# A fused attention, routing and expert kernel: VectorE's order in a pair of blocks, shared value copies, early transposes, a held routing

## The chip, the cores and the metric

The kernel runs on one core of a Trainium2 chip. The core has five engines that run beside each other: TensorE (PE in the profile, with its weight loads as PEld), VectorE (DVE), ScalarE (ACT), GpSimd (POOL) and SyncE (SP, which here issues transfers). [...] The metric is device time in microseconds, the median of several executions. [...]

## What is computed

Three stages, one after the other:

```python
scores = q @ k.T / 8 + bias            # 4 batches x 8 heads, 768 rows, head size 64
keep   = (first 8 keys) | (own and 95 keys before)
x      = softmax(where(keep, scores, -1e9)) @ v        # as 3072 rows of 512

logits = x @ w_gate                    # 8 experts
order  = argsort(-logits.flatten())    # greedy: best pair first,
...                                    # each expert takes 384 rows
y[mask_e] = relu(x[mask_e] @ w1[e]) @ w2[e]

out = relu(y @ w_in)**2 @ w_out        # 512 -> 2048 -> 512
```

All of it in float32. In the expert stages each operand is split into a high and a low part, and three products take the place of one.

## The kernel before

**Attention.** `attention` goes through 48 pairs of units (4 batches, 4 pairs of heads, 6 blocks of 128 rows; a unit is one block of one pair of heads). The loop `for p in range(NP)` is software pipelined by hand: what it writes down is the order on every engine, since nothing reorders it later. In pair p, with u = 2p: `qk` forms the scores of units u and u+1 on TensorE (L288); `smax` (L298, two instructions per unit) adds the bias and takes the row minimum on VectorE; `sexp` (L306) takes the exponentials on ScalarE; `tr_pe` and `tr_ev` (L315, L320) transpose those of the pair before on TensorE and copy them out of PSUM on ScalarE, in two PSUM buffers `pt0` and `pt1`; `av` (L331) multiplies those of two units earlier with the values into the one PSUM buffer `px0`; and `av_ev` (L336) copies that into `xT` on VectorE.

Tasks are hung into the pairs by tables: `PEF` and `PEL` on TensorE, `DV` on VectorE, `D` for stores. In six pairs for each of the first three batches, `nat_pe` transposes a block of `xT` back (L377) into the bank `mi`, `nat_ev` scales it on VectorE (L380), and `nat_st` stores 128 finished rows of x to `xd` in HBM. Four other pairs of a batch hold the gate logits (`gate_mm` to `gate_red`). `side` is called twice at the end of a pair: it advances the conversion of the last stage's weights, which arrive as 64-bit numbers (`convert`: two GpSimd instructions L928 and L930, two VectorE instructions L932 and L934 for each half matrix), and the preparation of the routing (`prepare`, L579 to L588). VectorE's order in a pair is thus: `smax` twice, the value copy, the pair's other tasks, `side`.

**Routing.** `Router.stage` picks the 384 rows of one expert: it finds a threshold by rounds of compare and count (VectorE compares into `r_ge`, TensorE counts into `r_ps`), then turns the chosen rows into a list of indices: `onehot` on VectorE (tile `r_O`, shown as `c_q<-prow,r_sb`), `place` on TensorE (shown as `r_ps<-va,c_q`). Stage 0 runs alone, ahead of the experts; stages 1 to 7 run beside them.

**Experts.** `ffn` gathers the rows of an expert (`c_xg<-xd,idx`), transposes them (`xtp`), splits them into high and low parts (`parts`: ScalarE casts, VectorE subtracts, tile `c_XT`), and runs the expert (`hg`, `y`) and the last stage (`hg`, `o`) on TensorE, weights being split by ScalarE (`wh`) and GpSimd (`wl`). From stage 0 on, the order on each engine is set while the program is built: `Sched` holds generators that yield the engine they want next, or a function that must become true first, and `Clock` keeps an estimate of when each engine is free (`free`) and when a tile is there (`there`). All these instructions carry line L77. The last batch's six blocks of rows are `tail` tasks of this scheduler: each makes its transposes (into `s0`, `s1`), scales them with eight ScalarE instructions (`xn`) and stores them, between the rounds of routing stage 0.

Of the kernel before, what the change touches and what calls it, by code (L numbers as in the profile page):

```python
# [6 lines left out]
FT = mybir.dt.float32  # L7
# [3 lines left out]
PELAG, PEL = 1.6, 2  # L11
# [106 lines left out]
class Sched:  # L118
# [34 lines left out]
    def run(self, until=None):  # L153
        while self.tasks and not (until and until()):
            best = None
            hold = HOLD if self.busy() else HOLD0
            S, U = [], []
            self.moved = False
            for t in list(self.tasks):
                if t not in self.tasks: continue  # L160
                s = self.start(t)
                if s:
                    S.append((t, s[0], s[1]))
                    U.append(S[-1])

                    if isinstance(t[3], str) and ">" in t[3]: U.append((t, "DVE", s[1] + float(t[3].split(">")[1])))
            if not S:
                assert self.moved, [(t[2].__name__, t[2].gi_frame.f_lineno) for t in self.tasks]
                continue
            for t, eng, s in S:  # L170

                p = t[5] if eng == "PE" else t[0]
                held = (eng != "PE" or not self.busy()) and any(e == eng and u[0] < p and s <= q < s + hold for u, e, q in U)
                key = (held, round(s/0.05), p, t[1])
                if best is None or key < best[0]: best = (key, t)
            self.advance(best[1])
# [6 lines left out]
BIG = 3.0e38  # L183
MASK8 = -8.0e9
FAR = 2.0**43
ND = 1
def first_keys(n_global):

    return 8*max((n_global + 7)//8, 1)
# [17 lines left out]
def tags(name, n):  # L207
    return tuple(f"{name}{i}" for i in range(n))

def attention(tc, sb, pp, q, k, v, wgb, xd, L, n_global, n_local, ident, prepare, beside=()):  # L210
# [4 lines left out]
    nc = tc.nc  # L215
    V, ACT, G, PE, SP = nc.vector, nc.scalar, nc.gpsimd, nc.tensor, nc.sync
    B, HP, NB = 4, 4, 6
# [28 lines left out]
    own, g = rel[:, W-128:W], n_global  # L246
# [15 lines left out]
    T0 = sb.tile([128, 8, 128], FT, "T0")  # L262
# [14 lines left out]
    st, XT, PX = {}, {}, {}  # L277
# [56 lines left out]
    def av_ev(p, copy=V.tensor_copy):  # L334
        b, hp, i = units[2*p]
        copy(XT[b][:, hp, i*128:i*128+256], PX[0])  # L336
    PEF, PEL, DV, D = {}, {}, {}, {}
    def at(where, t, f, *a):
        where.setdefault(t, []).append((f, a))
    GM = {}  # L340
# [20 lines left out]
    def gate_red(b, i0, n, tag="gt"):  # L361
        t = sb.tile([128, n*HP, 2, 8], FT, "gt", (tag,))
        p = GM.pop((b, i0)).rearrange("p i (c a e) -> p (i c) a e", c=HP, e=8)[:, :, 0:2]
        R = RC[:, b, i0:i0+n].rearrange("p i (c a) -> p (i c) a", c=HP)
        V.tensor_tensor(t, p, R[:, :, :, None].to_broadcast([128, n*HP, 2, 8]), op=OP.mult)
        i0 += b*NB
        V.tensor_reduce(L[:, i0:i0+n], t.rearrange("p (i c) a e -> p i e (c a)", c=HP), axis=AX.X, op=OP.add)
        if b < B-1: ready.append((i0, n))
    def parts():
        while True:  # L370
            part = ready.pop(0) if ready else None
            if part == (): return
            yield part
    def nat_pe(b, i, nc=nc):
        GM[3] = pp.tile([128, 512], FT, "nat", ("mi",) if b < B-ND else ("s0", "s1"))
        for hp in range(HP):
            nc.tensor.transpose(GM[3][:, hp*128:hp*128+128], XT[b][:, hp, i*128:i*128+128], ident)  # L377
    def nat_ev(b, i):
        x = GM['x', b, i] = sb.tile([128, 8, 64], FT, "xn", tags('wo', 3))
        V.tensor_tensor(x, GM[3].rearrange("p (h d) -> p h d", h=8), RC[:, b, i, :, None].to_broadcast([128, 8, 64]), op=OP.mult)  # L380
    def nat_act(b, i, p, nc=nc):
        GM['x', b, i] = sb.tile([128, 8, 64], FT, "xn", tags('wo', 3))
        for h in range(8):
            nc.scalar.activation(GM['x', b, i][:, h], p[:, h*64:h*64+64], AF.Copy, scale=RC[:, b, i, h:h+1])
# [3 lines left out]
    for b in range(B - 1):  # L388
        t0 = 12*b + 14
        for f in range(2):  # L390
            d = t0 + 2*f
            if f == 0: at(DV, d, recip, b, 0, NB)
            at(PEL, d, gate_mm, b, 3*f, 3, "mi"); at(DV, d, gate_ev, b, 3*f, 3)
            at(PEF, d+1, gate_tr, b, 3*f, 3, "mi"); at(DV, d+1, gate_red, b, 3*f, 3)
        for i in range(NB if b < B-ND else 0):
            d = t0 + 4 + i
            at(PEF, d, nat_pe, b, i); at(DV, d, nat_ev, b, i); at(D, d, nat_st, b, i)
    for h in range(2, 8): at(DV, h-2, table, h)
    prep = prepare(parts())
    def side(t):  # L400
        for g, n, t0 in beside:
            if t >= t0 and t % n == 0: next(g, None)
        next(prep, None)
    def run(tasks, p):
        for f, a in tasks.get(p, ()): f(*a)
    for p in range(NP):
        u = 2*p
        qk(u)
        qk(u+1)
        n = p // 3  # L410
        if p % 3 == 2 and n + 3 < NQ: load_qk(n+3)
        if p >= 1:
            tr_pe(u-2)
            tr_pe(u-1)
        run(PEF, p)
        smax(u)
        sexp(u)
        if p >= 1: tr_ev(u-2)
        if p >= 2:
            av(u-4)  # L420
            av(u-3)
            if p % 3 == 1 and n + 1 < NQ and n >= 1: load_v(n+1)
        smax(u+1)
        sexp(u+1)
        if p >= 1: tr_ev(u-1)
        run(PEL, p)
        if p >= 2: av_ev(p-2)
        run(DV, p)
        run(D, p)
        side(u)  # L430
        side(u+1)

    b, u = B - 1, 2*NP
    tr_pe(u-2)
# [13 lines left out]
    gate_tr(b, 0, 4, "s0")  # L448
    gate_ev(b, 4, 2, "gs", ACT.copy)
    gate_tr(b, 4, 2, "s2")  # L450
    gate_red(b, 0, 4, "T0")
    next(prep, None)
    gate_red(b, 4, 2)
    ready.extend([(b*NB, NB), ()])
    for _ in prep: pass

    def rows(b, i):
        def steps(nc):
            yield "PE"
            nat_pe(b, i, nc)  # L460
            p = GM[3]
            yield "ACT"
            nat_act(b, i, p, nc)
            yield "SP"
            nat_st(b, i, nc)
        return steps
    return [rows(b, i) for b in range(B-ND, B) for i in range(NB)]

SENT = -1.0e29
BIG = 3.0e38  # L470
# [5 lines left out]

ONE23, MASK = 0x4b000000, 0xffffffff
WMODE = (2,3,4,5,6)

class Router:  # L480

# [109 lines left out]
    def stage(self, s, wp, ps, idx, eidx):  # L591
# [235 lines left out]
        for i, g in enumerate(gs):  # L827
            for h in g:
                onehot(h)
                if h < g[-1] or s == 0 and h < 1: yield ("DVE", sb)  # L830
            if s == 0 and i < 1: continue
            if s == 0: g = gs[i-1]
            yield ("PE", Os[g[-1]], va)
            for h in g: place(h)
            if i < len(gs) - 1: yield ("DVE", sb)
# [121 lines left out]
def ffn(tc, pools, router, ident, xd, wab, wov, wol, out, tail, wih, wil):  # L957
# [58 lines left out]
    def routing(s):  # L1016
        idx[s] = sb.tile([128, 3], I32, "idx", tags("idx", 8))
        eidx[s] = sb.tile([1, 1], I32, "eidx", tags("eidx", 8))
        for r in router.stage(s, wp, rps, idx[s], eidx[s]):
            if r == "e": known.add(s)  # L1020
            elif r == "idx": done.add(s)
            elif r == "soon": soon.add(s)
            else: yield r
        if s + 1 < NE: S.add(routing(s+1), PR[s+1], -1)
# [270 lines left out]
    def rows(g):  # L1295
        yield from g
        n["rows"] += 1
# [177 lines left out]
```

## Time and profile before

| | us |
|---|---|
| median of 3 runs | 1094.42 (1093.69 to 1094.96) |
| the profiled execution's own time | 1095.79 |
| its span, first to last instruction | 1094.0 |
| TensorE busy | 1039.1 (95%) |
| VectorE busy | 717.7 (66%) |
| ScalarE busy | 427.7 (39%) |
| GpSimd busy | 414.9 (38%) |

The profiled execution took 1.79 us more than its span and 1.37 us more than the median. TensorE's share is high throughout, but matrix instructions overlap and their ends are modelled, so a busy TensorE need not be one at its peak. The stages lie as follows: attention until about 181 us, the last blocks and routing stage 0 until about 218.5 us, the gather and the first split until 230 us, and then the eight experts until 1085 us, with the last rows written by 1094 us.

### The profile page before, as it was taken

The page shows a single profiled execution, that of the slowest core. Times are in us where ns is not written, and L with a number is a line of the kernel's source. Part 1 is how long each engine was busy: PE and PEld are TensorE (multiplying, and loading weights), DVE is VectorE, ACT ScalarE, POOL GpSimd, SP SyncE. Part 2 cuts the span into 40 slices and gives each one's busy share as a digit, 9 for nine tenths or more (in the row PEclk, how much of TensorE's full clock was granted, in tenths as well). Part 3 has the DMA queues.
Part 4 walks back from the last instruction along what each step waited for, and adds up shares of the span by engine and source line. Part 5 has one row for each costly group of instructions (what it writes and reads, how often), then busy time and mean ns, then how long its engine had stood idle before and what let it go on. Part 6 is the DMA issues. An engine that isn't in the chain of part 4 may idle for free.

```text
span 1094.0 us, 19130 instructions
## 1 busy us (share of the span) xinstructions
PE 1039.1 (95%) x6599; PEld 919.8 (84%) x6599; DVE 717.7 (66%) x2633; ACT 427.7 (39%) x1087; POOL 414.9 (38%) x458
## 2 busy tenths in 40 slices
PE   8999897589999999999999999999999999999997
PEld 5666665479888988998999889989988999899996
DVE  6888887664489868878887788778876122232322
ACT  7877775533344332332233223322332233223221
POOL 2645550274264443434344335433542355006001
PEclk9999999599999999999999999999999999999999
DMA  8879863652232232323332333223322234123021
GB/s 297 310 271 348 281 245 134 219 163 92 87 125 85 80 126 87 106 72 102 96 107 78 97 87 106 86 88 97 117 87 76 88 116 144 59 62 123 29 68 58
DMA packets 53043, 139.53 MB, mean 128 GB/s; under 512 B 6225, under 2 KB 6609, under 8 KB 52945
## 3 DMA queue, kind: packets, MB, share of 16 engines
q1 hardware_dynamic: 49104, 125.72, 34.2%
q0 software_dynamic: 3840, 12.59, 3.5%
q8 instruction: 52, 0.85, 0.3%
q14 instruction: 47, 0.38, 0.1%
HBM read 117.31 MB, written 20.97 MB: 126 GB/s over the span
## 4 chain that ended last, share of the span: by engine, by line
PE 69%; DVE 10%; issue 2%; ACT 1%; DMA 0%; POOL 0%; POOLq 0%; DVEq 0%; ACTq 0%
PE hg L77 33%; PE o L77 21%; PE y L77 12%; DVE r_ge L77 3%; PE r_ps L77 2%; DVE c_q L77 2%; DVE r_tc L77 1%; DVE r_t L77 1%; DVE va L77 0%; DMA c_xg<-xd,idx 0%; DVE r_th L77 0%; DVE r_pre L77 0%; DVE r_fc L77 0%; DVE c_XT L77 0%; PE xtppt L77 0%
## 5 line engine op out<-in xcount | busy, mean ns | idle before, releaser
L77 PE MATMUL hg<-c_XT,wi 128*128 128x384 f32 x1536 | 291.8, 338 | 0.0
L77 PEld LDWEIGHTS hg<-c_XT,wi 128*128 128x128 f32 x1536 | 270.5, 188 | 9.4
L77 POOL TENSOR_TENSOR wl<-c_T,wh 128x512 fp32r<-128x512 f32 x128 | 167.8, 1326 | 104.5 <-ACT wh L77 104.2
L77 ACT ACTIVATE c_gs<-hg 128x384 f32<-128x384 f32 x128 | 62.8, 491 | 291.9 <-PE hg L77 291.9
L77 DVE TENSOR_SCALAR_CACHE_REDUCE r_ge<-r_wv,r_th 128x192 bf16<-128x192 f32 x350 | 143.8, 411 | 9.5
L77 DVE SCALAR_TENSOR_TENSOR c_q<-hg,c_gs 128x384 f32<-128x384 f32 x112 | 62.3, 556 | 123.5 <-ACT c_gs L77 123.5
L77 PE MATMUL hg<-c_XT,wh 128*128 128x384 f32 x512 | 134.4, 344 | 2.7 <-DVE c_XT L77 2.4
L306 ACT ACTIVATE P<-ns,nm 128x232 f32<-128x232 f32 (+1 forms) x192 | 89.4, 467 | 44.9 <-DVE nm L298 44.6
L77 PE MATMUL o<-wol,c_k 128*128 128x512 f32 x264 | 104.4, 395 | 0.0
L77 PEld LDWEIGHTS hg<-c_XT,wh 128*128 128x128 f32 x512 | 93.4, 190 | 5.3 <-DVE c_XT L77 4.1
L77 ACT CAST wh<-c_T 128x512 fp32r<-128x512 f32 x128 | 75.8, 617 | 38.8 <-DMA c_T<-in_wab 28.5
L77 POOL DMA_INDIRECT out<-c_xg,idx x24 | 23.7, 986 | 168.4 <-DVE c_xg L77 151.3
L77 PE MATMUL hg<-c_XT,wl 128*128 128x384 f32 x256 | 86.7, 339 | 0.0
L77 POOL TENSOR_TENSOR c_q<-c_q,c_q 128x384 fp32r<-128x384 f32 x30 | 31.4, 1045 | 119.2 <-ACT c_q L77 73.8
L77 PE MATMUL y<-c_k,wh 128*128 128x384 f32 x256 | 71.8, 341 | 0.0
L315 PE MATMUL pt<-ident,P 128*128 128x128 f32 x352 | 57.2, 290 | 13.0 <-ACT PT L320 12.8
L315 PEld LDWEIGHTS pt<-ident,P 128*128 128x128 f32 x352 | 38.1, 143 | 35.0 <-ACT PT L320 26.0
L77 ACT CAST c_k<-c_q 128x384 fp32r<-128x384 f32 x88 | 45.2, 513 | 51.3 <-DVE c_q L77 50.6
L298 DVE CUSTOM_DVE_ANT_0 ns<-s,T 128x232 f32<-128x232 f32 (+1 forms) x192 | 61.4, 373 | 2.1 <-PE s L288 2.1
L77 POOL TENSOR_TENSOR c_v<-c_q,c_k 128x384 fp32r<-128x384 f32 x30 | 30.6, 1022 | 77.9 <-PE o L77 53.0
L288 PE MATMUL s<-kr,qr 64*128 64x232 f32 (+1 forms) x384 | 54.3, 386 | 5.6 <-DMA kr<-in_k 4.4
L77 POOL TENSOR_TENSOR c_k<-c_q,c_k 128x384 fp32r<-128x384 f32 x30 | 31.1, 1036 | 70.9 <-ACT c_k L77 45.0
(276 smaller groups left out, 2051.6 us busy)
## 6 DMA issues: line engine op xcount, KB each, us to landing
wol<-wol SPq DMA_DIRECT2D x128, 256.0 KB, 2.6
c_T<-in_wab SPq DMA_DIRECT2D x64, 512.0 KB, 3.5
raw<-in_m SPq DMA_DIRECT2D x32, 512.0 KB, 7.2
vr<-in_v SPq DMA_DIRECT2D x16, 704.0 KB, 5.4
xd<-xn SPq DMA_DIRECT2D x24, 256.0 KB, 2.6
kr<-in_k SPq DMA_DIRECT2D x15, 404.0 KB, 7.1
qr<-in_q SPq DMA_DIRECT2D x15, 384.0 KB, 6.9
wov<-ct SPq DMA_DIRECT2D x16, 256.0 KB, 5.3
```

The source lines that it names most:

```text
L77: return f(*a, **k)
L288: PE.matmul(s[a][:, :n], qr[h, i*128:i*128+128], kr[h, c0:c0+n], start=True, stop=True)
L298: V.tensor_tensor_reduce(out=ns[:, a, :n], in0=s[a][:, :n], in1=tb, scale=-0.125, scalar=BIG, op0=OP.add, op1=OP.min, accum_out=nm[:, a:a+1])
L306: ACT.activation(P[:, a, :n], ns[:, a, :n], AF.Exp, bias=nm[:, a:a+1], scale=-1.0, accum_out=s)
L315: PE.transpose(pt[:, c, a], P[:, a, c*128:c*128+128], ident)
```

## The change

Four things are changed.

1. In a pair of attention blocks, VectorE does `nat_ev`, its store and the two `side` calls before the value copy `av_ev`; the tasks in `DV` (reciprocals, the gate's copies and sums, the bias tables) come behind it. In pairs with an odd number ScalarE makes the value copy, at the end of its own pair.
2. The last batch's 24 transposes are made right behind the gate's, ahead of routing stage 0, into six PSUM banks; only the scaling and the stores are left to the scheduler.
3. Routing stage 1 starts only when the first expert's rows are split (`parted["x", 0] == 4`).
4. In stages 1 to 7 a `place` is put into TensorE's order only when the scheduler's estimate has TensorE free `LATE` = 2.0 us or more after the one-hot tile is there.

```diff
-    PEF, PEL, DV, D = {}, {}, {}, {}
+    PEF, PEL, DF, DV, D = {}, {}, {}, {}, {}
...
-    def nat_pe(b, i, nc=nc):
-        GM[3] = pp.tile([128, 512], FT, "nat", ("mi",) if b < B-ND else ("s0", "s1"))
+    def nat_pe(b, i, tag="mi"):
+        GM[3] = pp.tile([128, 512], FT, "nat" + tag, (tag,))
...
-        for i in range(NB if b < B-ND else 0):
+        for i in range(NB):
             d = t0 + 4 + i
-            at(PEF, d, nat_pe, b, i); at(DV, d, nat_ev, b, i); at(D, d, nat_st, b, i)
+            at(PEF, d, nat_pe, b, i); at(DF, d, nat_ev, b, i); at(D, d, nat_st, b, i)
...
         run(PEL, p)
-        if p >= 2: av_ev(p-2)
-        run(DV, p)
+        run(DF, p)
         run(D, p)
         side(u)
         side(u+1)
+        if p >= 2: av_ev(p-2, ACT.copy if p % 2 else V.tensor_copy)
+        run(DV, p)
...
     gate_tr(b, 4, 2, "s2")
-    gate_red(b, 0, 4, "T0")
+    nat = []
+    for i in range(NB):
+        if i == 5: gate_red(b, 0, 4, "T0")
+        nat_pe(b, i, ("pt0", "pt1", "px1", "s1", "mi", "s0")[i])
+        nat.append(GM[3])
...
-    def rows(b, i):
+    def rows(i):
         def steps(nc):
-            yield "PE"
-            nat_pe(b, i, nc)
-            p = GM[3]
             yield "ACT"
-            nat_act(b, i, p, nc)
+            nat_act(b, i, nat[i], nc)
...
             if s == 0: g = gs[i-1]
+            else: yield lambda: nc.free["PE"] > nc.there("PE", Os[g[-1]]) + LATE
             yield ("PE", Os[g[-1]], va)
...
     def routing(s):
...
+        if s == 1: yield lambda: parted["x", 0] == 4
         for r in router.stage(s, wp, rps, idx[s], eidx[s]):
```

The instruction order shows three places. The first is VectorE in pair 42 of the attention loop, an even pair with a block of finished rows; `ISA` is `smax`. Before:

```order
L298 ISA nm 128x1
L336 COPY xT<-px 128x256
L380 TENSOR_TENSOR xn<-nat,RC 128x512
L932 SCALAR_TENSOR_TENSOR ct<-cab,ct 128x512
L581 TENSOR_TENSOR r_t_170<-L,r_m 128x24
L582 TENSOR_TENSOR r_ge<-r_m,th_219 128x48
L934 SCALAR_TENSOR_TENSOR ct<-raw_2306,ct 128x512
L584 TENSOR_TENSOR r_t_170<-r_t_170,w_180 128x24
L298 ISA ns,nm<-s,T_128 128x232
```

And with the change:

```order
L297 ISA nm 128x1
L379 TENSOR_TENSOR xn<-natmi,RC 128x512
L938 SCALAR_TENSOR_TENSOR ct<-cab,ct 128x512
L593 TENSOR_TENSOR r_oh<-r_t_168,r_code 128x24
L940 SCALAR_TENSOR_TENSOR ct<-raw_2305,ct 128x512
L584 TENSOR_REDUCE r_m<-L 128x3
L335 COPY xT<-px 128x256
L297 ISA ns,nm<-s,T_128 128x232
```

The value copy has moved from the front to the back; in odd pairs VectorE has none, and ScalarE's order has a `COPY xT<-px` behind the pair's second `PT<-pt`.

The second place is VectorE at the first expert, where its rows are split (`c_XT<-xtp`, four instructions); `rcol` is the last instruction of routing stage 0, `r_m` the first of stage 1, and `c_q<-hg` the first activation. Before:

```order
L77 TENSOR_SCALAR rcol<-r_ps 128x1
L77 TENSOR_REDUCE r_m<-L 128x24
L77 TENSOR_TENSOR r_t_3576<-L,r_m 128x192
L77 TENSOR_TENSOR r_t_3576<-r_t_3576,w_180 128x192
L77 TENSOR_TENSOR c_XT_3025<-xtpmi,c_XT_3025 128x384
```

And with the change:

```order
L77 TENSOR_SCALAR rcol<-r_ps 128x1
L77 TENSOR_TENSOR c_XT_3055<-xtpmi,c_XT_3055 128x384
L77 TENSOR_TENSOR c_XT_3055<-xtps_3539,c_XT_3055 128x384
L77 TENSOR_TENSOR c_XT_3055<-xtps_3540,c_XT_3055 128x384
L77 TENSOR_TENSOR c_XT_3055<-xtps_3541,c_XT_3055 128x384
L77 TENSOR_REDUCE r_m<-L 128x24
L77 TENSOR_TENSOR r_t_3588<-L,r_m 128x192
L77 SCALAR_TENSOR_TENSOR c_q_3035<-hg,c_q_3035 128x384
L77 TENSOR_TENSOR r_t_3588<-r_t_3588,w_178 128x192
```

The four splits stand ahead of routing stage 1's first instructions instead of behind three of them, and the first `r_t` stands right ahead of the first activation.

The third place is TensorE at the first `place` of routing stage 3 (`r_ps<-va`); `o` and `hg` are products of the last stage. Before:

```order
L77 MATMUL o<-wol,c_k_3011 128x512
L77 MATMUL o<-c_k_3009,c_v_3012 128x512
L77 MATMUL o<-c_k_3009,c_k_3011 128x512
L77 MATMUL o<-wol,c_k_3011 128x512
L77 MATMUL o<-c_k_3009,c_v_3012 128x512
L77 MATMUL hg<-c_XT_3025,wi_810 128x384 x12
L77 LDWEIGHTS c_q_3006
L77 MATMUL r_ps<-va,c_q_3006 128x6
```

And with the change:

```order
L77 MATMUL o<-wol,c_q_3035 128x512
L77 MATMUL o<-c_v_3042,c_q_3035 128x512
L77 MATMUL hg<-c_XT_3055,wi_1410 128x384 x12
L77 MATMUL o<-c_v_3043,c_k_3039 128x512
L77 MATMUL o<-wol,c_k_3039 128x512
L77 MATMUL o<-c_v_3043,c_k_3040 128x512
L77 MATMUL o<-c_v_3043,c_k_3039 128x512
L77 MATMUL o<-wol,c_k_3039 128x512
L77 MATMUL o<-c_v_3043,c_k_3040 128x512
L77 LDWEIGHTS c_q_3036
L77 MATMUL r_ps<-va,c_q_3036 128x6
```

Six more products stand ahead of the first `place` (30 behind the last product of the step before it, instead of 24), and the second `place` stands 18 products behind the first instead of 9.

## Rows read from the trace of the kernel before

**Rows 1.** Stretches: length, busy PE, PEld, DVE, ACT, POOL; granted clock, DMA share, GB/s.
```profile
6.00:150.00 144.00, 133.35 (x1267) 98.11 (x1267) 123.34 (x504) 110.60 (x397) 72.11 (x102) 1.00 0.87 311
150.00:181.00 31.00, 27.75 (x269) 20.54 (x268) 26.68 (x104) 22.84 (x82) 9.56 (x12) 1.00 0.38 137
190.50:218.50 28.00, 15.82 (x234) 12.38 (x230) 17.55 (x91) 14.69 (x57) 6.32 (x5) 0.50 0.62 209
230.00:238.00 8.00, 7.95 (x53) 6.98 (x54) 3.66 (x9) 3.03 (x6) 4.14 (x3) 0.79 0.35 110
238.00:1084.60 846.60, 836.70 (x4653) 769.83 (x4653) 528.27 (x1884) 269.30 (x534) 305.72 (x285) 1.00 0.29 92
```

**Rows 2.** Waits from 6 to 181 us: us in total, times, longest.
```profile
DVE xT L336 <- PE px L331: 22.0, 30, 1.8
PE pt L315 <- ACT PT L320: 12.4, 24, 0.9
```

**Rows 3.** Timeline of VectorE, pairs 32 and 33: start, us, instruction, [idle before <- releaser].
```profile
121.31 0.40 DVE L298 CUSTOM_DVE_ANT_0 ns<-s,T 128x232 f32<-128x232 f32 x1
...
123.35 0.43 DVE L336 COPY xT<-px 128x256 f32<-128x256 f32 x1 [0.67 <-PE px L331]
...
124.29 0.93 DVE L932 SCALAR_TENSOR_TENSOR ct<-cab,ct 128x512 int32<-128x512 int32 x1
...
126.92 0.42 DVE L336 COPY xT<-px 128x256 f32<-128x256 f32 x1
...
129.18 0.39 DVE L298 CUSTOM_DVE_ANT_0 ns<-s,T 128x232 f32<-128x232 f32 x1
```

**Rows 4.** Timelines of ScalarE and TensorE in the same two pairs.
```profile
124.13 0.56 ACT L320 COPY PT<-pt 128x512 f32<-128x512 f32 x1
...
122.42 0.88 PE L331 MATMUL px<-PT,vr 128*64 128x128 f32 x12
...
125.24 0.60 PE L377 MATMUL nat<-ident,xT 128*128 128x128 f32 x4
125.77 1.09 PE L331 MATMUL px<-PT,vr 128*64 128x128 f32 x16
```

**Rows 5.** Groups from 6 to 186 us, the value copy: busy, mean ns | idle before.
```profile
L336 DVE COPY xT<-px 128x256 f32<-128x256 f32 x47 | 19.8, 421 | 22.1 <-PE px L331 22.0
```

**Rows 6.** Timeline of TensorE, counts of routing stage 0.
```profile
190.30 0.30 PE L77 MATMUL r_ps<-r_ge,r_oh 128*8 128x16 bf16 x6 [2.27 <-DVE r_oh L588]
...
192.85 0.75 PE L77 MATMUL r_ps<-r_ge,r_oh 128*8 128x16 bf16 x24
...
207.21 0.75 PE L77 MATMUL r_ps<-r_ge,r_oh 128*8 128x16 bf16 x24 [0.86 <-DVE r_ge L77]
...
209.34 0.75 PE L77 MATMUL r_ps<-r_ge,r_oh 128*8 128x16 bf16 x24 [0.87 <-DVE r_ge L77]
```

**Rows 7.** Timeline of VectorE, routing stage 0 and the first split.
```profile
198.15 1.11 DVE L77 SCALAR_TENSOR_TENSOR r_th<-r_dg,r_pre 128x16 int32<-128x16 int32 x1
...
202.04 0.17 DVE L77 SCALAR_TENSOR_TENSOR r_th<-r_dg,r_pre 128x16 int32<-128x16 int32 x1
...
223.87 5.12 DVE L77 TENSOR_TENSOR r_t<-L,r_m 128x192 f32<-128x192 f32 x1
229.03 0.36 DVE L77 TENSOR_TENSOR r_t<-r_t,w 128x192 f32<-128x192 f32 x1
229.30 0.55 DVE L77 TENSOR_TENSOR c_XT<-xtpmi,c_XT 128x384 fp32r<-128x384 f32 x1
```

**Rows 8.** Timeline of GpSimd in the same stretch.
```profile
222.59 4.96 POOL L77 TENSOR_TENSOR wl<-c_T,wh 128x512 fp32r<-128x512 f32 x4
227.51 1.26 POOL L77 TENSOR_TENSOR c_clo<-c_ct,c_v 128x512 fp32r<-128x512 f32 x1
```

**Rows 9.** Timeline of TensorE, the first expert's first products with the split's low parts.
```profile
229.91 2.72 PE L77 MATMUL hg<-c_XT,wh 128*128 128x384 f32 x6 [1.89 <-DVE c_XT L77]
```

**Rows 10.** Waits of TensorE from 230 us to the end.
```profile
PE r_ps L77 <- DVE c_q L77: 6.8, 9, 1.9
```

More of the change, by code (lines that the diff above doesn't have):

```diff
@@ L185 @@
 FAR = 2.0**43
-ND = 1
 def first_keys(n_global):
@@ L373, in parts @@
             yield part
-    def nat_pe(b, i, nc=nc):
-        GM[3] = pp.tile([128, 512], FT, "nat", ("mi",) if b < B-ND else ("s0", "s1"))
+    def nat_pe(b, i, tag="mi"):
+        GM[3] = pp.tile([128, 512], FT, "nat" + tag, (tag,))
         for hp in range(HP):
-            nc.tensor.transpose(GM[3][:, hp*128:hp*128+128], XT[b][:, hp, i*128:i*128+128], ident)
+            PE.transpose(GM[3][:, hp*128:hp*128+128], XT[b][:, hp, i*128:i*128+128], ident)
     def nat_ev(b, i):
@@ L380, in nat_ev, with nat_act @@
         V.tensor_tensor(x, GM[3].rearrange("p (h d) -> p h d", h=8), RC[:, b, i, :, None].to_broadcast([128, 8, 64]), op=OP.mult)
-    def nat_act(b, i, p, nc=nc):
+    def nat_act(b, i, p, nc):
         GM['x', b, i] = sb.tile([128, 8, 64], FT, "xn", tags('wo', 3))
@@ L466, in rows @@
         return steps
-    return [rows(b, i) for b in range(B-ND, B) for i in range(NB)]
+    return [rows(i) for i in range(NB)]
 SENT = -1.0e29
@@ L478 @@
 WMODE = (2,3,4,5,6)
+LATE = 2.0
 class Router:
```

## The prediction

> **What bounds the kernel now.** I read the busy time by stretch first, then the waits, then the timelines. From 238 us to the end of the last product TensorE is busy 836.70 of 846.60 us at the full clock [rows 1]: there the product count is the bound, and only stalls of TensorE can be won. Ahead of that no engine is full. From 6 to 181 us TensorE is busy 133.35 + 27.75 = 161.1 of 175 us, VectorE 150.0, ScalarE 133.4 [rows 1], and the largest wait of VectorE is for the value product, 22.0 us in 30 waits [rows 2]. From 190.5 to 218.5 us TensorE works 15.82 of 28.00 us at a granted clock of 0.50, its lower level [rows 1]: this is routing stage 0, a chain of short steps between TensorE and VectorE. The reader should see that each stretch has a bound of its own, and that the four edits go to four stretches.
>
> **The value copy.** VectorE's loop goes over two pairs. Pair 32 starts at 121.31, pair 34 at 129.18, 7.87 us later [rows 3]. In between ScalarE ends its second PT copy at 124.13 + 0.56 = 124.69, TensorE follows with the transposes and the block's rows (125.24 + 0.60 = 125.84) and with the value product (125.77 + 1.09 = 126.86) [rows 4], and VectorE's copy starts at 126.92 and pair 34 2.26 us behind it, after the copy, the scaled rows and two conversions [rows 3]. In the new order the scaled rows and conversions hang on the transposes alone: 124.69 - 121.31 = 3.38, plus 125.84 - 124.69 = 1.15, plus the same 2.26, is 6.79 us, or 1.08 less; where the copy lies with ScalarE, up to 0.42 less again [rows 5]. That would be some 0.6 us a pair and 26 us over 42 pairs. It can't all come: TensorE has only 175 - 161.1 = 13.9 us idle, which is the upper end. The lower end from mechanism alone is 0 (the wait was slack); a loss is a rival below. I take 9, about two thirds of the idle time: at 166 us TensorE is busy 97%, VectorE (150.0 less 23 copies of 0.421 [rows 5]) 84%, ScalarE (133.4 and 23 copies of as much, at most: its PT copy, twice the size, takes 0.56 [rows 4]) 86%, and the DMA share of 0.87 up to 150 us [rows 1] rises to about 0.92; none is full, but TensorE is near it. The 23 copies on ScalarE cost nothing by themselves: they stand behind the PT copy, which ends 3.38 us into a pair, when the value product of that pair is mostly done (pair 32's ends at 122.42 + 0.88 = 123.30, 1.99 us into it [rows 4]); without this cover ScalarE would wait and the next exponentials with it. The stores leave earlier on SP's queue, ahead of the weights that `side` asks for; each is one of many transfers there, and I cost that at nothing as long as the DMA share stays below 1.
>
> **The early transposes.** Six groups now stand ahead of routing stage 0's first count. TensorE has a hole of 2.27 us there, until VectorE has `r_oh` [rows 6]. At the full clock a group occupies about 0.53 us (0.60 long, the next product 0.53 behind it [rows 4]), so six take 3.2 and the 24 counts 0.75 more: the first count ends at about 187.4 + 3.2 + 0.8 = 191.4 instead of 190.6, a loss of 0.8. In return the rounds lose their company. From 192.85 to 209.34 six rounds take 16.49 us, 2.75 each; the last, undisturbed one takes 209.34 - 207.21 = 2.13 [rows 6]. That is 3.7 us of excess, of which 0.94 is one `r_th` of 1.11 us where another takes 0.17 [rows 7], beside a GpSimd subtraction that stays. So 2.8 go, and 0.7 with the group between the first count and its product (two half-clock lengths of 0.53, less 0.35 that TensorE waited anyway). Net gain 2.6. Bounds: 4.5 if GpSimd's subtractions, which move with ScalarE's casts, miss VectorE's sensitive steps, and a loss of 1 if they meet two more.
>
> **The held routing stage.** Before, `r_t` of stage 1 takes 5.12 us where its twin takes 0.36 [rows 7]; it ends with GpSimd's run of 4.96 and 1.26 us [rows 8]. [...] What is late next is the first activation, which `r_t` now precedes: by then GpSimd's run is nearly over (TensorE wants the low parts at 229.91 - 1.89 = 228.0 [rows 9]; I estimate that four splits of 0.55 [rows 7] end then, `r_t` starts near 228.5, and GpSimd's run ends at 227.51 + 1.26 = 228.77 [rows 8]), and TensorE has 12 products of the next block, some 2 us at 0.18 us each (846.60 us for 4653 instructions [rows 1]), to do meanwhile. [...]
>
> **The held places.** TensorE waits 6.8 us in nine waits for one-hot tiles, at most 1.9 us [rows 10]. Now the scheduler wants 2.0 us of its own estimate between tile and product, more than any of these waits. I take 6 of the 6.8; bounds 7.5 (each restart costs something too) and 2 (VectorE lags the estimate by more than before, and the waits return). The routing gets later by it: stage 6's last `place` now stands 156 products ahead of the transposes of its rows instead of 264 (counted in the order); at 0.18 us a product that is 28 us, much more than the first expert's rows need from the end of stage 0 at 218.5 to the first product with a low part at 229.91 [rows 9]. Cost nothing, and some us per stage if that lead were gone.
>
> **Sum.** 9 + 2.6 + 3.2 + 6 = 20.8 us off the profiled execution's 1095.79, which gives 1075.0; the median of the runs lies 1.37 lower, so 1073.6.
>
> **Rivals.**
> - *The wait was slack.* TensorE or ScalarE takes VectorE's place at once, and attention gains 2 instead of 9: 1080.6. For it: ScalarE's copies already hold TensorE 12.4 us in 24 waits [rows 2]. Against it: these waits end with ScalarE, which itself waits for VectorE's minima in the same loop. Seen by px waits gone and ScalarE or the transposes waiting instead. 15%.
> - *The clock under the transposes.* Six groups run at the lower level, 6.3 us instead of 3.2, and the first count is 3.1 later still: 1076.7. The stretch that follows is at 0.50 already [rows 1]; against it, the same transposes run at 1.00 among the attention's products. [...] 12%.
> - *The hold doesn't hold.* VectorE's one-hots meet GpSimd and come later than 2 us behind the estimate; 1 of the 6 is won: 1078.6. 12%.
> - *Slower: the copy comes too late.* The value product has one PSUM buffer. In pair 32 it is done at 123.30 and wanted again at 125.77, 2.47 us later [rows 4]; now the scaled rows and two conversions come first (2.26 less the copy's 0.42 is 1.84 us [rows 3]). VectorE is free at 123.35 - 0.67 = 122.68 [rows 3], so the copy ends at about 124.9, in time by 0.8. A conversion that meets a GpSimd subtraction of 1.26 us [rows 8] turns that into 0.4 late, two into 1.7. It decides when the lost time passes 0.8: with a mean of 1.1 us late in each of 23 even pairs TensorE loses 25 us, and the other three edits win 11.8: 1107.9. Against it: a pair's conversions are rarely both held, and a late VectorE delays the next scores too, which moves the time at which the buffer is wanted. 4%.
>
> **How the numbers follow.** The forecast as worked out has 55%, the rivals 15, 12, 12 and 4, 2 is left for what I don't see. The bounds alone sum to 1065 at best (13.9 + 4.5 + 3.6 + 7.5 = 29.5 off) and 1093 at worst (0 - 1 + 0 + 2 = 1 off); all ends at once are unlikely, so the range is 1064 to 1085, which also takes in the first three rivals. A measurement of this kernel can tell about 0.2%, 2.2 us, from no change; of the cases only the fourth rival and part of the rest do not beat that: faster 0.93, same 0.03, slower 0.04.
>
> **What would show it.** VectorE's waits for px gone or under 5 us, and the first count of routing stage 0 at about 182 instead of 190 us; rounds of 2.1 us with TensorE on nothing else; no stall at the first expert's low parts and a clock of 1.00 behind it; TensorE's waits for one-hot tiles near zero, with 840 us or less from there to the last product. Wrong would be: an unchanged start of routing stage 0, a TensorE that waits for the value copy in even pairs, a long `r_t` in front of the first activation that TensorE waits for, or gathers that TensorE waits for in the later experts.

## The result, and the profile after

The changed kernel takes 1068.85 us (median, 1067.96 to 1069.49), beside 1094.14 us for the kernel before on the same chip: a ratio of 0.977, with a 95% interval from 0.975 to 0.978, or 25.3 us less. The forecast was 1073.6 us. The profiled execution took 1069.27 us with a span of 1067.3 us, 26.7 us less than the span before.

Following the same instructions in both traces shows where the 26.7 us came from:

| instruction | before | after | gained so far | in this part | forecast |
|---|---|---|---|---|---|
| first transpose of the last gate (`gn`) | 186.62 | 170.43 | 16.2 | attention: 16.2 | 9 |
| last `idx` of routing stage 0 | 218.35 | 199.70 | 18.65 | early transposes: 2.5 | 2.6 |
| first expert's first product | 226.25 | 207.64 | 18.6 | | |
| first second product (`y`) | 235.01 | 212.05 | 23.0 | held routing: 4.4 | 3.2 |
| end of the span | 1094.0 | 1067.3 | 26.7 | held places: 3.7 | 6 |

The sum was 20.8 us; what came in these two traces is 5.9 us more. Attention brought 7.2 us more than forecast and the held routing 1.2 more; the held places brought 2.3 less. The stretches after, with the columns of [rows 1]:

```profile
6.00:150.00 144.00, 139.07 (x1392) 103.59 (x1394) 135.52 (x537) 125.17 (x451) 82.44 (x111) 1.00 0.91 326
150.00:164.80 14.80, 14.36 (x147) 11.10 (x142) 12.28 (x48) 13.59 (x50) 1.88 (x2) 1.00 0.43 140
171.14:173.85 2.71, 2.71 (x26) 2.54 (x24) 2.53 (x9) 2.07 (x11) 0.00 (x0) 1.00 0.02 6
209.25:215.00 5.75, 5.75 (x34) 5.74 (x34) 4.78 (x9) 3.66 (x7) 4.67 (x4) 1.00 0.59 183
215.00:1057.80 842.80, 835.94 (x4673) 767.38 (x4672) 528.09 (x1884) 269.24 (x534) 308.35 (x287) 1.00 0.30 94
```

In attention (the first two rows, against the first two of [rows 1]) TensorE is busy 153.43 of 158.8 us. Its idle time fell from 13.9 to 5.4 us, and its busy time for the same products by 7.7 us. The third row is the 24 early transposes, at a granted clock of 1.00 throughout; the lowest that the traces of before and after show is 0.50. The fourth is the first expert behind the split, at 1.00 where [rows 1] has 0.79 for the same work. The waits from 6 to 164.8 us (in total, times, longest; compare [rows 2]):

```profile
ACT P L305 <- DVE nm L297: 19.7, 30, 1.9
PE pt L314 <- ACT PT L319: 4.2, 9, 0.7
DVE xT L335 <- PE px L330: 1.7, 4, 0.8
PE px L330 <- DVE xT L335: 0.6, 1, 0.6
```

VectorE's 22.0 us of waits for the value product are down to 1.7. TensorE's waits for ScalarE fell from 12.4 to 4.2 with them, although ScalarE has more to do: these waits hung on VectorE's wait. The last row is the price of the later copy, one wait of 0.56 us in one pair.

Routing stage 0, TensorE's timeline:

```profile
173.32 0.60 PE L376 MATMUL nats<-ident,xT 128*128 128x128 f32 x4
173.85 0.75 PE L77 MATMUL r_ps<-r_ge,r_oh 128*8 128x16 bf16 x24
...
176.17 0.75 PE L77 MATMUL r_ps<-r_ge,r_oh 128*8 128x16 bf16 x24 [1.09 <-DVE r_ge L77]
...
178.29 0.75 PE L77 MATMUL r_ps<-r_ge,r_oh 128*8 128x16 bf16 x24 [0.86 <-DVE r_ge L77]
...
180.75 0.75 PE L77 MATMUL r_ps<-r_ge,r_oh 128*8 128x16 bf16 x24 [1.20 <-DVE r_ge L77]
```

The wait of 2.27 us for `r_oh` [rows 6] is filled with transposes. Rounds are 2.12 us, or 2.46 where an `r_th` on VectorE takes 0.51 us instead of 0.17; the last one is 3.19, with an `r_th` of 1.24. The first expert, VectorE and GpSimd:

```profile
207.62 0.56 DVE L77 TENSOR_TENSOR c_XT<-xtpmi,c_XT 128x384 fp32r<-128x384 f32 x1 [3.66 <-ACT c_XT L77]
208.09 1.48 DVE L77 TENSOR_TENSOR c_XT<-xtps,c_XT 128x384 fp32r<-128x384 f32 x3
209.49 0.34 DVE L77 TENSOR_REDUCE r_m<-L 128x24 f32<-128x192 f32 x1
209.86 0.51 DVE L77 TENSOR_TENSOR r_t<-L,r_m 128x192 f32<-128x192 f32 x1
...
203.93 4.96 POOL L77 TENSOR_TENSOR wl<-c_T,wh 128x512 fp32r<-128x512 f32 x4
208.85 1.29 POOL L77 TENSOR_TENSOR c_clo<-c_cab,c_v 128x512 fp32r<-128x512 f32 x1
```

The four splits, which take one input from PSUM (where TensorE's results lie), take 0.56 and 1.48 us beside GpSimd; in the kernel before, behind the end of GpSimd's run, they take 0.55 and 1.48. The `r_t` of 5.12 us [rows 7] now starts when GpSimd's run is nearly over, and takes 0.51. From 215 us on, the waits of [rows 10] are gone, but TensorE has others:

```profile
PE y L77 <- DVE c_q L77: 3.6, 3, 1.5
PE r_ps L77 <- DVE r_t L77: 2.0, 2, 1.1
PE hg L77 <- DVE c_XT L77: 1.0, 1, 1.0
```

### The profile page after: what moved, and what is told of

It is laid out like the page before. It is cut to its first block, busy times and chain, and to the rows that moved or that the text cites. A ratio compares the mean times of both kernels' runs of the same rounds, so it can differ in the third digit from the quotient of the medians.

```text
span 1067.3 us, 19117 instructions
## 1 busy us (share of the span) xinstructions
PE 1025.2 (96%) x6599; PEld 911.1 (85%) x6599; DVE 711.8 (67%) x2610; ACT 433.3 (41%) x1110; POOL 418.6 (39%) x458
## 4 chain that ended last, share of the span: by engine, by line
PE 77%; DVE 15%; ACT 3%; issue 2%; DMA 1%; POOL 0%; SPq 0%; POOLq 0%; DVEq 0%; ACTq 0%
PE hg L77 33%; PE o L77 24%; PE y L77 9%; DVE r_ge L77 5%; PE r_ps L77 2%; ACT P L305 2%; PE px L330 2%; PE pt L314 2%; PE s L287 2%; DVE ns L297 1%; DVE r_th L77 1%; DVE r_fc L77 1%; DVE r_tc L77 1%; DVE r_pre L77 1%; ACT PT L319 1%
## 5 line engine op out<-in xcount | busy, mean ns | idle before, releaser
L77 PE MATMUL hg<-c_XT,wh 128*128 128x384 f32 x512 | 132.0, 339 | 1.3 <-DVE c_XT L77 1.0
L314 PE MATMUL pt<-ident,P 128*128 128x128 f32 x352 | 53.6, 287 | 4.7 <-ACT PT L319 4.6
L77 ACT ACTIVATE c_k<-hg 128x384 fp32r<-128x384 f32 x40 | 19.6, 491 | 90.1 <-PE hg L77 86.5
```

The source lines that it names most:

```text
L77: return f(*a, **k)
L314: PE.transpose(pt[:, c, a], P[:, a, c*128:c*128+128], ident)
```

## The experiments

Three questions were open: why attention gave 16.2 us where TensorE had 13.9 us idle; what each edit is worth by itself; and whether the three new kinds of waits belong to the held places. Times are medians; the kernel before took 1095.0, 1095.3 and 1095.2 us in the three sets of runs, and each gain is taken against its own set. A trace is one execution of its kernel.

**One edit at a time, attention.** The first kernel has only the first edit. The second has its order without the sharing, the third its sharing without the order:

```diff
 # the new order alone, behind side(u+1)
+        if p >= 2: av_ev(p-2)
 # the sharing alone, in the old place
-        if p >= 2: av_ev(p-2)
+        if p >= 2: av_ev(p-2, ACT.copy if p % 2 else V.tensor_copy)
```

> The kernel before with the first edit alone (VectorE's order in a pair, and odd pairs' value copy on ScalarE). The traces of before and after say that the stretch up to the last pair's bias instruction became 16.2 us shorter: theory one, all of that is this edit, gives 1094.1 - 16.2 = 1078 us. Theory two, the prediction's own cap (TensorE's idle time in the stretch, 13.9 us at the most, 9 taken), gives 1080 to 1085 us and would need another edit to explain the rest. In the trace theory one expects VectorE's waits for the value product below 5 us and TensorE's busy time between 6 us and the end of attention some 7 us lower than the 161.1 us of before; theory two expects that busy time unchanged.

> The new order alone: VectorE keeps all 47 value copies, but makes them behind the scaled rows, the store and the two conversion steps. If the order of VectorE is what mattered (the prediction's 1.08 us of a two-pair loop of 7.87, the larger of its two numbers), at least two thirds of the 16.2 us come: 1079 to 1084 us. If the work taken off VectorE is what mattered, no more than 4 us come: 1090 us or above. If the copy now comes too late for the single buffer of the value product (the prediction's fourth rival, here with nothing to relieve VectorE), it is slower than 1094 us, with TensorE waiting for the copy in most pairs.

> The sharing alone: in odd pairs ScalarE makes the value copy, in even pairs VectorE makes it in its old place, ahead of the scaled rows and conversions. If VectorE's wait for the value product is the whole matter, the sharing takes away about half of these waits (22.0 us in 30), and half of the gain comes: about 1086 us. If it is VectorE's load and not the order, nearly the whole gain comes: 1078 to 1081 us. If the order is the matter and the even pairs' wait simply stays, little comes: 1090 us or above.

Measured: 1079.72 us for the whole edit (15.3 less; ratio 0.986, 0.985 to 0.988), 1083.50 for the order alone (11.5 less; 0.990, 0.989 to 0.992), 1091.39 for the sharing alone (3.6 less; 0.997, 0.996 to 0.998). The trace of the whole edit decides between its two theories. VectorE's waits for the value product are 1.3 us there, and TensorE's busy time in attention is 8.0 us lower than the 161.1 of before, as theory one wanted:

```profile
6.00:164.80 158.80, 153.10 (x1536) 114.54 (x1537) 147.84 (x584) 139.03 (x501) 84.20 (x113) 1.00 0.87 310
```

The waits of the order alone, from 6 to 164.85 us, and below them those of the sharing alone, from 6 to 176 us:

```profile
ACT P L306 <- DVE nm L298: 27.6, 36, 1.7
...
PE pt L315 <- ACT PT L320: 6.0, 11, 0.8
...
DVE xT L336 <- PE px L331: 1.5, 4, 0.6
...
PE px L331 <- DVE xT L336: 0.7, 2, 0.4
```

```profile
DVE xT L336 <- PE px L331: 19.3, 20, 2.0
...
PE pt L315 <- ACT PT L320: 10.6, 21, 0.8
```

So the order is three quarters of it: the wait leaves VectorE although VectorE still makes all copies. The two parts add up to the whole within 0.2 us. With the sharing alone the even pairs' waits stay, 19.3 us in 20. Even with every copy late and on VectorE, TensorE waits for the copy only 0.7 us in all; the rival of the late copy falls with this run.

Where the gain beyond the idle time came from shows in TensorE's groups over attention (busy, mean ns of one | idle before), before and after:

```profile
L315 PE MATMUL pt<-ident,P 128*128 128x128 f32 x348 | 56.5, 290 | 12.6 <-ACT PT L320 12.4
L288 PE MATMUL s<-kr,qr 64*128 64x232 f32 (+1 forms) x376 | 52.7, 383 | 1.9 <-DVE nm L298 1.0 <-DMA kr<-in_k 0.8
L331 PE MATMUL px<-PT,vr 128*64 128x128 f32 x672 | 46.8, 279 | 0.0
```

```profile
L314 PE MATMUL pt<-ident,P 128*128 128x128 f32 x348 | 53.0, 287 | 4.4 <-ACT PT L319 4.2
L287 PE MATMUL s<-kr,qr 64*128 64x232 f32 (+1 forms) x376 | 48.8, 379 | 0.7 <-DVE nm L297 0.7
L330 PE MATMUL px<-PT,vr 128*64 128x128 f32 x672 | 46.8, 280 | 0.6 <-DVE xT L335 0.6
```

The counts are the same and the mean of one hardly moves (290 to 287, 383 to 379 ns), but the busy time of these two groups falls by 3.5 and 3.9 us; that of the value product, which hardly waited in either, stays at 46.8. Busy time counts each stretch once, and the records of matmuls that follow close on each other overlap: 376 times 383 ns would be 144 us, not 52.7. So a matmul that comes a little late need not leave idle time: the record of the one before can cover the hole. Here, by this reading, 7.4 us of such short holes stood under "busy". The waits of the weight loads agree, which are listed by themselves: those for `PT` fell from 25.4 to 11.4 us and those for the minima from 8.4 to 2.0.

**The early transposes alone.**

> The early transposes alone. The prediction gives 2.6 us off, 1091.5 us; the traces of before and after show 2.5 us for routing stage 0. The clock rival (transposes at the lower level) gives 1094.6 us. In the trace: the six groups of transposes at a granted clock of 1.00, the first count about 0.8 us later than before, the rounds at 2.1 us except those in which VectorE's step meets a GpSimd instruction.

Measured: 1096.77 us, 1.8 us *slower* (ratio 1.0024, 1.0012 to 1.0035), which neither theory expected. In its trace routing stage 0 does end 2.6 us earlier, `idx` at 215.76 instead of 218.35, just as forecast. What follows takes the gain back (VectorE, GpSimd, TensorE):

```profile
220.41 0.34 DVE L77 TENSOR_REDUCE r_m<-L 128x24 f32<-128x192 f32 x1
220.79 5.59 DVE L77 TENSOR_TENSOR r_t<-L,r_m 128x192 f32<-128x192 f32 x1
...
227.93 0.55 DVE L77 TENSOR_TENSOR c_XT<-xtpmi,c_XT 128x384 fp32r<-128x384 f32 x1
...
219.99 4.94 POOL L77 TENSOR_TENSOR wl<-c_T,wh 128x512 fp32r<-128x512 f32 x4
224.89 1.26 POOL L77 TENSOR_TENSOR c_clo<-c_cab,c_v 128x512 fp32r<-128x512 f32 x1
...
228.07 0.75 PE L77 MATMUL r_ps<-r_ge,r_oh 128*8 128x16 bf16 x24 [4.72 <-DVE r_ge L77]
228.75 0.69 PE L77 MATMUL hg<-c_XT,wh 128*128 128x384 f32 x1
```

The earlier routing let the scheduler put stage 1's first count ahead of the first expert's products on TensorE. That count hangs on `r_t`, which ends at 226.38 us, 0.23 behind GpSimd's run, so TensorE stands still for 4.72 us and the first product comes at 228.75 instead of 226.25, the first `y` at 235.42 instead of 235.01. The rest of the loss lies behind that: from the first `y` to the end it takes 860.5 us instead of 859.0. TensorE's granted clock is 0.91 there from 490 to 510 us, behind a wait of 1.89 us for a one-hot tile, where the kernel before has 1.00. A mean of 0.91 over 20 us is 3.6 us at 0.50, and in the kernel before a group of four transposes takes 1.12 us at 0.50 (at 190.53 us) instead of 0.60 at 1.00 [rows 4]; so that is some 1.8 us lost, an estimate. The 24 transposes ran at a granted clock of 1.00 here too, 2.72 us for all six groups.

**The held routing alone and the held places alone.** Each is the one added condition of the diff, in the kernel before.

> The held routing stage 1 alone. The prediction gives 3.2 us off, at most 3.6 (1090.9, at the least 1090.5); the traces of before and after show 4.35 us between the first product and the first activation's product, which would be 1089.8 us. Rival: the next r_t meets another run of GpSimd and most is given back, 1093 us or above. In the trace: the subtractions that split the first expert's rows stand ahead of r_t, TensorE doesn't wait for them, and its clock stays at 1.00 behind them.

> The held places alone. The prediction gives 6 us off, 1088.1 us. The accounting from the traces of before and after (what is left of 26.7 us after 16.2, 2.5 and 4.35) gives 3.7 us off, 1090.4 us, with TensorE's waits for one-hot tiles gone but new waits for activations (3.6 us in 3) and for r_t (2.0 us in 2) in their place. If those new waits belong to the held places, they show in this trace too; if they belong to the other edits, this run gains the full 6.

Measured: 1092.09 us for the held routing (3.2 less; ratio 0.997, 0.996 to 0.999), and 1085.53 for the held places (9.8 less; 0.992, 0.990 to 0.993), more than either expectation. The latter's first second product comes at 234.0 us in its trace instead of 235.0, of which 0.7 us came before routing stage 0 had ended and so not by this edit. From there to the end it took 850.4 us instead of 859.0, and its list of TensorE's waits there has one row left, against 9.9 us in the same list of before:

```profile
PE r_ps L77 <- DVE r_t L77: 2.0, 2, 1.1
```

**The changed kernel without one of these, or without both.** The square is made by taking the two added lines out:

```diff
-            else: yield lambda: nc.free["PE"] > nc.there("PE", Os[g[-1]]) + LATE
...
-        if s == 1: yield lambda: parted["x", 0] == 4
```

> The changed kernel with the places not held. If the places' share is 3.7 us, 1072.6 us; if it is the predicted 6, 1074.9 us; if the held places bring nothing in the company of the other edits, 1068.9 us. In the trace TensorE's waits for one-hot tiles should be back at some 7 us, and the waits for activations and r_t tell whether the hold makes them.

> The changed kernel with routing stage 1 not held. If the hold's share is what the traces show, 4.35 us, 1073.2 us; by the prediction's 3.2, 1072.1 us. [...] Rival (r_t was long by chance of one execution): r_t takes 0.4 us or one GpSimd instruction's 1.26 us, and the time is 1069 us.

> The changed kernel without the hold of stage 1 and without the held places, so that the first two edits are left. With the three runs of the changed kernel that have both (1068.9), only the hold (1075.4) and only the held places (1069.1) it makes a square. If hold and held places were independent, 1075.6 us. If the sum of the edits made one at a time holds (15.3 off for the first, 1.8 on for the second), 1081.6 us; then the held places are worth 12 us without the hold and 6.5 with it, and the hold 6 us without the held places and nothing with them.

| with the first two edits | no held places | held places |
|---|---|---|
| no held routing | 1082.07 | 1069.10 |
| held routing | 1075.42 | 1068.85 |

The held places are worth 13.0 us without the held routing and 6.6 with it; the held routing 6.7 without the held places and 0.3 with them. The four times come from three sets of runs. With each gain taken against its own set (13.1, 19.9, 26.2 and 25.3) these are 13.1, 5.4, 6.8 and -0.9 us, so beside the held places the held routing shows no gain. The two are not independent, and the sum over edits made alone came true (1081.6 expected for the corner without both). In the kernel without the held routing, `r_t` is long again (VectorE, GpSimd, TensorE):

```profile
205.24 5.60 DVE L77 TENSOR_TENSOR r_t<-L,r_m 128x192 f32<-128x192 f32 x1
...
204.46 4.94 POOL L77 TENSOR_TENSOR wl<-c_T,wh 128x512 fp32r<-128x512 f32 x4
209.35 1.26 POOL L77 TENSOR_TENSOR c_clo<-c_cab,c_v 128x512 fp32r<-128x512 f32 x1
...
212.53 0.75 PE L77 MATMUL r_ps<-r_ge,r_oh 128*8 128x16 bf16 x24 [4.83 <-DVE r_ge L77]
```

So `r_t` was not long by chance of one execution, but the 1072.1 to 1073.2 us expected did not come: the first `y` stands at 219.87 us, 7.8 later than with the hold, but from there to the end it takes 847.1 us instead of 855.3. With the hold, 7.8 us are gained at the first expert (0.8 of them before it, since routing stage 0 began that much earlier in that execution), and 8.1 us are lost afterwards. Some 0.8 us of the loss is only counted differently: without the hold, stage 1's first count stands ahead of the first `y`.

**Where it is lost.** Of those 8.1 us, 5.6 are TensorE's waits (6.6 us in the list above against 1.0 without the hold) and 0.8 are that count; the other 1.7 stand in no listed wait. The wait at 553 us, on VectorE, with TensorE's product below it:

```profile
549.16 1.29 DVE L77 SCALAR_TENSOR_TENSOR r_th<-r_dg,r_pre 128x8 int32<-128x8 int32 x1
550.48 1.22 DVE L77 TENSOR_TENSOR r_pre<-r_th,jw 128x8 int32<-128x8 int32 x1
...
552.87 0.55 DVE L77 SCALAR_TENSOR_TENSOR c_q<-hg,c_q 128x384 fp32r<-128x384 f32 x1
...
553.47 0.44 PE L77 MATMUL y<-c_q,wh 128*128 128x384 f32 x1 [1.05 <-DVE c_q L77]
```

Two routing steps on a few numbers (an `r_th` takes 0.17 us undisturbed [rows 7]) take 1.29 and 1.22 beside two GpSimd subtractions that start at 549.13 and take 2.55 together. The activation stands behind them in VectorE's order and comes too late. The waits at 660 and 767 us have the same cause (an `r_th` of 1.21 and one of 1.28 us, each beside GpSimd), and at 298 us TensorE waits for an `r_t` itself: an earlier `r_t` of that stage, at 292.99 us, took 2.89 us beside a run of three GpSimd instructions. If that is a matter of where the routing's steps happen to lie against the experts, shifting them without touching anything else should change it. Three kernels do so:

```diff
-        if s == 1: yield lambda: parted["x", 0] == 4
+        if s == 1: yield lambda: n["y"] >= 4        # and, in another, >= 2
...
-LATE = 2.0
+LATE = 3.0
```

> The changed kernel with routing stage 1 held longer: until four groups of the first expert's second products are in TensorE's order, instead of until its rows are split. Without any hold the stretch from the first second product (y) to the end took 847.2 us, with the hold 855.3, of which 6.6 us are waits of TensorE for an activation, an r_t and a split that stand behind routing steps on VectorE. Theory one: these waits come from where the routing's steps happen to lie against the experts and GpSimd; then a later hold, which shifts all stages, changes them, and as the first y still starts near 212 us, the time falls to between 1060 and 1066 us if they go, or stays near 1069 if others come. Theory two: a hold costs by itself, since every later stage is late; then a longer hold is slower, 1071 us or above, with waits for gathers or rows.

> The changed kernel with routing stage 1 held until two groups of second products are in TensorE's order. As for the hold to four groups: theory one, 1060 to 1066 us if the waits for activations go, else near 1069; theory two, between the changed kernel's 1068.9 us and the time with the longer hold, in order of the hold's length.

> The changed kernel with LATE = 3.0 instead of 2.0. It also shifts the stages, by moving each place further behind. Theory one (the lie of the routing against the experts decides): a time that differs from 1068.9 us by 1 to 6 us in either direction, with the waits for the activation at 553, 660 and 767 us gone or moved, and none for one-hot tiles. Theory two (2.0 us is enough, and a later place costs by itself): 1069 to 1072 us, the same waits at the same places.

Measured: 1072.50 us with the hold to four groups (ratio 0.980, 0.978 to 0.981), 1065.55 with two (0.973, 0.972 to 0.974), and 1064.41 with `LATE` = 3.0 (0.972, 0.971 to 0.974). The last two beat the changed kernel, whose interval begins at 0.975. The waits of TensorE with `LATE` = 3.0, from 212 us:

```profile
PE hg L77 <- DVE c_XT L77: 1.3, 1, 1.3
PE y L77 <- DVE c_q L77: 0.8, 1, 0.8
PE y L77 <- DVE c_k L77: 0.4, 2, 0.2
PE o L77 <- POOL c_v L77: 0.2, 1, 0.2
```

A longer hold is not slower in order of its length (1068.9, then 1065.6, then 1072.5), so its length alone doesn't decide. The longest one has the time that theory two gave it, but not by the waits that theory two named: it has no wait for gathers but 2.2 us for one `r_t`, 1.8 for activations and 1.7 for a `wol` of GpSimd. Over these kernels the time from the first `y` to the end goes with the waits that the trace lists there:

| kernel | first `y` | from there to the end | TensorE's listed waits |
|---|---|---|---|
| before | 235.0 | 859.0 | 9.9 |
| first two edits | 218.9 | 860.5 | 12.5 |
| no held places | 214.0 | 861.3 | 10.5 |
| changed kernel | 212.1 | 855.3 | 6.6 |
| hold to four groups | 210.8 | 858.1 | 6.2 |
| hold to two groups | 212.9 | 851.8 | 3.1 |
| `LATE` = 3.0 | 210.6 | 850.6 | 2.7 |
| held places alone | 234.0 | 850.4 | 2.0 |
| no held routing | 219.9 | 847.1 | 1.0 |

The difference of the last two columns is 846 to 852 us. Part of what is left is TensorE's clock. Three of the traces have a stretch of lower granted clock right behind such waits: the granted clock is 0.83 from 580 to 590 us without the held places (behind a wait of 1.89 us), 0.91 from 310 to 330 us with the held places alone (behind waits of 1.11 and 0.89), and 0.89 from 290 to 320 us with the hold to four groups (waits of 1.70 and 2.19, at 304 and 311 us), where the changed kernel has 1.00. If these means are made up of 0.50 and 1.00, and TensorE's work takes twice as long at 0.50 (by the kernel before, where the first expert's product behind the one at 232.42 us starts 0.32 us later, at 0.50, and that behind the one at 234.31 us 0.17 later, at 1.00), that is 1.7, 1.8 and 3.3 us, an estimate. Not every such wait does it: the trace of the kernel before has one of 1.9 us, and its clock stays at 1.00 from 238 us on. Without these parts, and with the 0.8 us of the first count added for the two kernels that make it ahead of the first `y` (the first two edits, and no held routing), the difference is 847 to 849 us for all nine. That is bookkeeping over one execution each; that the lie of the routing makes the waits rests on the timelines at 553, 660 and 767 us.

## Why the prediction was right, and where not

**The value copy: the mechanism right, the term too small (9, measured 15.3 alone and 16.2 in the trace).** The step that failed is "It can't all come: TensorE has only 175 - 161.1 = 13.9 us idle, which is the upper end". Idle time is not an upper end: TensorE's busy time fell by 7.7 us as well; by the reading above, these were holes shorter than a matmul's record. The working for two pairs gave 0.6 us a pair, and 26 in all; from the start of pair 2 to that of pair 47 a pair now takes 3.36 us instead of 3.71 (161.56 - 10.43 against 177.76 - 10.61, over 45), 0.35 less. The rival that the wait was slack (1080.6) fell: no other wait took its place. The late copy was seen once, and just in the pair that the working had used. VectorE in pair 32 after, which starts at 110.08:

```profile
112.28 0.98 DVE L938 SCALAR_TENSOR_TENSOR ct<-cab,ct 128x512 int32<-128x512 int32 x1
...
113.29 1.04 DVE L940 SCALAR_TENSOR_TENSOR ct<-raw,ct 128x512 int32<-128x512 int32 x1
...
114.81 0.41 DVE L335 COPY xT<-px 128x256 f32<-128x256 f32 x1
```

The two conversions take 0.98 and 1.04 us, beside GpSimd's two conversion steps, where those of pair 33 take 0.68 and 0.69; the copy starts 4.73 us into the pair, and TensorE waits 0.56 us for it: the fourth rival's mechanism, with another GpSimd instruction than the subtraction that it named, once in 46 pairs and at half a microsecond.

**The early transposes: the term right (2.6, measured 2.6 in the trace of the edit alone and 2.5 in the whole), but only under the cover of other edits.** The prediction's own parts, 2.8 and 0.7 less 0.8, make 2.7 and not 2.6. The prediction priced it as if what follows routing stage 0 kept its order. Alone, it lost 1.8 us, and its trace shows stage 1's count in front of the experts; that the whole came out close owes something to luck. The loss of 0.8 us at the first count was only 0.2: from the gate's last transposes to its end it took 3.98 us before, 4.18 with the edit alone and 4.17 in the whole, since groups of transposes alone follow each other in 0.44 us, not 0.53. Three rounds of the changed kernel still met a GpSimd subtraction (an `r_th` of 0.51, 0.52 and 1.24 us), where the forecast had one and the lower bound three; the kernel before had two, of 1.11 and 0.46. The clock rival (1076.7) fell by the third row of the stretches after: granted clock 1.00. In this stretch of 24 transposes, 2.7 us long, the clock did not fall; no run here has a longer one.

**The held routing: 3.2 forecast, 3.2 measured alone, 4.4 in the trace.** The 3.2 was the author's estimate: no run shows the parts of this term, and in their place the traces show two. TensorE's wait of 1.89 us [rows 9] is gone; and behind its end at 229.91 the products up to the first `y` took 5.10 us, with a granted clock of 0.50 from 230.84 to 234.26, and now take 2.80 at 1.00, 2.3 less. By the estimate above the clock is 1.7 of these 2.3; the weight loads also waited three more times for a split there (0.28, 0.28 and 0.18 us). That it is worth 6.7 us beside the early transposes and nothing that shows beside the held places was not foreseen. On the cause, all eight kernels without the hold agree: `r_t` takes 4.64 to 5.73 us and ends 0.2 us behind the last of GpSimd's five subtractions. In the four shown or named here it ends at 228.99, 226.38, 210.84 and, with the first edit alone, after 5.42 us at 212.34; the subtractions end at 228.77, 226.15, 210.61 and 212.11. In the kernel before, `r_t` starts as the first of the five ends, at 223.87 us, and stands beside the other four. The small `r_th` and `r_pre` at 549 us took 1.29 and 1.22 us, each about as long as one subtraction (2.55 for the two), and `r_t` on 192 numbers a partition took the rest of a run of 6.2 us; why they differ was not tried. The splits, whose other input is in PSUM, were not held up (0.56 us beside GpSimd, 0.55 without it).

**The held places: 6 forecast, 9.8 measured alone, 3.7 left in the whole.** All 6.8 us of waits for one-hot tiles went, as forecast, and so did waits for other tiles of the routing and for activations that stood in the same list (3.1 us), which the sum did not count; 2.0 us for an `r_t` came instead. The 9.8 is more than the upper bound of 7.5, which counted on the restarts of TensorE; no run shows what a restart costs by itself. In the whole, new waits of 6.6 us took part of it back; taking the held places out of the changed kernel costs 6.6 us, or 5.4 with each gain against its own set. Such a wait is the rival "the hold doesn't hold" in its mechanism (VectorE's routing steps meet GpSimd and come later than estimated), but it strikes the activations and not the one-hot tiles. Its time, 1078.6, was far off.

The forecast was thus 4.7 us high: one term 6 to 7 us too small, one 2 us too large in this company, the others close. That two of these errors have opposite signs is luck, and so is that the interplay of the edits, which the sum left out, took little from the whole: the four edits made alone add up to 26.5 us, and the whole gave 25.3. The list of what would show it came true in attention, at the first expert and for the one-hot tiles; the first count stands at 173.85 us rather than 182; and from 215 us to the last product it is 842.8 us, with the new waits in it, rather than 840 or less.

## What to carry to other kernels

A bound's idle time is not the most that removing a wait can win: compare a group's busy time with its count and the mean of one, since short holes can hide under overlapping records. Where an order is planned from estimates, an edit's price is that of its mechanism plus what it does to the order behind it; make each edit alone, and the pairs that touch the same stretch together, before adding terms. And a small instruction queued ahead of one that TensorE needs costs what it can wait for, not what it takes: here 0.17 us of work held an activation for over a microsecond.

## What the runs showed of the hardware

In all eight kernels without the hold, the `r_t` on VectorE that started beside a run of GpSimd subtractions, both its inputs in SBUF (the other on-chip memory), ended 0.2 us behind the last of them, after 4.64 to 5.73 us. Small instructions got in between the subtractions of a run: in the changed kernel, beside a run of three that starts at 654.70 us and takes 3.79, `r_tc`, `r_fc` and `r_th` took 1.01, 0.95 and 1.21 us and each ended within 0.1 us of the end of one subtraction; without GpSimd they take 0.19 and 0.17 (at 548.48 and 548.95 us) and 0.17 [rows 7]. The splits, with one input in PSUM, took 0.56 us beside GpSimd and 0.55 without it, and `r_m`, with a single input, 0.34 beside it, where `r_code` of the same shape takes 0.35 without it (at 296.30 us). But one input alone is no safe sign: in the kernel before, an `r_g<-r_U` on 24 numbers took 1.26 us at 213.28 us beside a GpSimd subtraction, and its twin right behind it 0.16. The second surprise is how much a shift of some microseconds in the routing decides: kernels that differ in one condition or one constant lie between 1064.4 and 1072.5 us, with the same number of matrix products and, but for a few, of instructions.
